# The pace of a frequency transform between the steps of a gated layer: a step clock that waits don't move, later ends for the first three transforms, and scatters of routing in threes

## The chip, the cores and the metric

One core of a Trainium2 chip runs the whole program in one launch. The metric is the device time of an execution in microseconds (us). The core has five engines that run side by side, each through its own list of instructions in order: TensorE (PE, matrix products), VectorE (DVE), ScalarE (ACT), GpSimd (POOL) and SyncE (SP, which here only issues DMAs). They wait for each other by semaphores. An instruction that waits holds everything behind it in its engine's list.

## The reference

The input x has 8 batches of 3072 tokens with 256 channels. Three stages follow each other:

```
X = rfft(x, axis=1)                       # along the tokens
Yr = Xr @ w_r - Xi @ w_i + b_r            # Yi the same with w_i, w_r, b_i
Y  = sign(Y) * max(|Y| - 0.01, 0)         # real and imaginary part by themselves
y  = irfft(Y)
z  = (sigmoid(y @ w_gate) * (y @ w_val)) @ w_out          # 256 -> 1536 -> 256
out = z; for tokens with z @ w_skip > 0:                  # routed to the best of 8 experts
    out += p_best * (relu(z @ w1[e]) @ w2[e])             # 256 -> 1024 -> 256
```

All matrix products are made of float16 high and low halves, three products for one.

## The kernel before

**Stages.** The program first sets up weights and makes the transform of batch 0 (the first 197 us). Then comes the main loop: 768 units, each one twelfth of the gated layer for one chunk of 384 tokens (8 batches x 8 chunks x 12). A unit is 12 matmuls for gate and value (L986, tile pg), the product of the two on DVE (h, then its low half hh), and 9 matmuls into the output (L1028, tile pz). After the loop come the experts' blocks (`Blocks`, tiles ph and py), 512 tokens or fewer at a time.

**What runs beside the units.** `moe_gen` yields once a unit. Between units, `build` gives turns to five other generators, its tasks:
- "attn": the transforms of batches 1 to 7 (`attn_gen`). Each has a stage of columns (x is scaled and split into xh, multiplied by c, stored through ah to asc) and one of 13 frequency groups (loaded as al; `freq` makes x, `mix` or `mix_pair` multiplies by wri and wse and shrinks, giving yn and by DMA yh, `inv` makes zh, stored to zsc).
- "y": `y_gen` finishes the inverse transform for one chunk, from zsc through zt, and leaves yT, which the gated layer's units of that chunk read.
- "route": `route` picks the experts of a batch's tokens and scatters an entry for each (the tile rent) into the list lst, 24 scatters a batch, by an indirect DMA that POOL issues (L1127). For the last batch it runs chunk by chunk, 3 scatters each; then come `full_table` and `rest_tables`, which say what the blocks work on.
- "prep": the experts' weights are scaled and split into float16 halves (pw, phl), 171 steps in all, the fill of the list lst among them.
- "start": the first blocks' loads, after the rest.

**What sets the order.** It is worked out while the program is built. Each task has a clock, counted in units. A step of a task may run when its clock is not past the unit; the one furthest behind goes first; and each unit has a budget of 2.0 us of estimated DVE and POOL or ACT work (BUDGET). After a step of "attn" its clock moves on by the step's estimated work times `span`, so that a transform should end 45 units (AHEAD) before its batch's own units begin. The other tasks move by a fixed number of units or by their work. A step may also set `k.due`, a unit before which its task isn't to go on: `settle` does (a maximum over all partitions is made by a matmul that rides with the next unit), and then the clock is raised to it, for "attn" as for the others.

When a task finds that what it needs isn't there, it names the other task, and `go` runs a step of that one at once, whatever budget or clock say. So y, when batch b isn't transformed (`while b not in k.made: yield "attn"`), and so `front` of the blocks, for a table.

The 8 chunks of y of a batch have due times too: LEAD and two chunks ahead of their use.

Of the kernel before, what the change touches and what calls it, by code (L numbers as in the profile page):

```python
# [16 lines left out]
NB, SEQ, D = 8, 3072, 256  # L17
# [6 lines left out]
NF = FF // 128  # L24
# [217 lines left out]
def task(gen):  # L242
    return [gen, []]


def step(k, r):

    k.V.sum = k.S.sum = k.T.sum = k.G.sum = 0.0
    todo, k.late = r[1], []
    for f in todo:  # L250
        f()
    got = next(r[0], -1)
    r[1] = k.late
    if got == -1 or isinstance(got, str):
        for f in r[1] if got == -1 else ():
            f()
        return got
    return max(k.V.sum + k.G.sum, k.S.sum)
# [647 lines left out]
def zt_load(k, b, c, boot=False):  # L906
    pool = k.sp0 if boot else k.yp
    zt = k.zt[b, c] = pool.tile([4 * NK, NJ, 2, D], F16, tag="zt", name=f"zt_{b}_{c}", bufs=1 if boot else 2)
    k.nc.sync.dma_start(zt, k.zsc[b][:, c * NJ:(c + 1) * NJ])
# [156 lines left out]
def route(k, b, t0, T):  # L1066

    nc, V, rp = k.nc, k.V, k.rp
    R = k.R[b][:, t0:t0 + T]
    L, S = R[:, :, 1:], R[:, :, 0]  # L1070
    tile_ = lambda tag, dt=F32, shape=None: rp.tile(shape or [128, T * NE], dt, tag=tag, name=f"{tag}_{b}_{t0}", bufs=1)
    tt = tile_("rt", shape=[128, 4, T])
    mx, sm, ac, gt = (tt[:, i] for i in range(4))
    et = lambda v: v.rearrange("p (e t) -> p e t", e=NE)
    te = lambda v: v.rearrange("p (e t) -> p t e", e=NE)
    bc = lambda v: v.unsqueeze(1).broadcast_to([128, NE, T])
    be = lambda v: v.unsqueeze(2).broadcast_to([128, NE, T])
    Le = L.rearrange("p t e -> p e t")
    dl, oh, w1, w2 = tile_("rdl"), tile_("roh"), tile_("rw1"), tile_("rw2")
    V.tensor_reduce(mx, L, axis=AX.X, op=ALU.max)  # L1080
    V.tensor_tensor(et(dl), Le, bc(mx), op=ALU.subtract)
    V.tensor_scalar(w1, dl, 0.0, None, op0=ALU.is_ge)
    k.S.activation(w2, dl, AF.Sigmoid)
    k.S.activation(dl, dl, AF.Sigmoid, scale=-1.0)
    yield
    V.reciprocal(dl, dl)
    V.tensor_tensor(dl, w2, dl, op=ALU.mult)
    V.tensor_tensor(et(w1), et(w1), be(k.rc[:, 0:NE]), op=ALU.mult)
    V.tensor_reduce(mx, te(w1), axis=AX.X, op=ALU.max)
    V.tensor_tensor(et(oh), et(w1), bc(mx), op=ALU.is_equal)  # L1090
    V.tensor_reduce(sm, te(dl), axis=AX.X, op=ALU.add)
    V.tensor_scalar(sm, sm, 1e-9, None, op0=ALU.add)
    V.reciprocal(gt, sm)
    V.tensor_scalar(ac, S, 0.0, None, op0=ALU.is_gt)
    oa = tile_("roa", F16)
    V.tensor_tensor(et(oa), et(oh), bc(ac), op=ALU.mult)
    yield
    ps = k.pa.tile([128, 512], F32, tag="pa", name="ps")
    W = T * NE
    nc.tensor.matmul(ps[:, :W], k.m16[:, 0], oa, start=True, stop=True)  # L1100
    nc.tensor.matmul(ps[:, W:2 * W], k.m16[:, 1], oa, start=True, stop=True)
    tot = tile_("rtot")
    V.tensor_copy(tot, ps[:, W:2 * W])
    V.tensor_tensor(w1, ps[:, :W], tot, op=ALU.subtract)
    yield
    V.memset(w2, 1.0)
    V.memset(et(w2)[:, :, 0:1], 0.0)
    V.tensor_tensor(et(tot)[:, :, 0], et(tot)[:, :, 0], k.base, op=ALU.add)
    inc = tile_("rdl")
    V.tensor_tensor_scan(inc, w2, tot, 0.0, op0=ALU.mult, op1=ALU.add)  # L1110
    V.tensor_copy(k.base, et(inc)[:, :, T - 1])
    yield
    V.tensor_tensor(w1, w1, inc, op=ALU.add)
    V.tensor_tensor(et(w1), et(w1), be(k.rc[:, NE:2 * NE]), op=ALU.add)
    V.tensor_tensor(w1, w1, oa, op=ALU.mult)
    V.tensor_reduce(sm, te(w1), axis=AX.X, op=ALU.add)
    yield
    V.tensor_scalar(ac, ac, -BIG, BIG, op0=ALU.mult, op1=ALU.add)
    idx = rp.tile([128, T], I32, tag="ridx", name="ridx", bufs=2)
    V.tensor_tensor(idx, sm, ac, op=ALU.add)  # L1120
    ent = rp.tile([128, T, 4], F32, tag="rent", name="rent", bufs=2)
    V.memset(ent[:, :, 3:4], 0.0)
    V.tensor_copy(ent[:, :, 0], gt)
    V.tensor_scalar(ent[:, :, 1:3], k.ids[:, t0:t0 + T, :], float(b * SEQ), None, op0=ALU.add)
    yield
    for t in range(T):
        nc.gpsimd.indirect_dma_start(  # L1127
            out=k.lst, out_offset=bass.IndirectOffsetOnAxis(ap=idx[:, t:t + 1], axis=0),
            in_=ent[:, t, :], in_offset=None, bounds_check=LROWS * BT - 1, oob_is_err=False,
        )  # L1130
        yield


def prep_gen(k):
# [247 lines left out]


def build(tc, d, nb=NB, nstat=NSTAT, dbg=None):
    PSTEP = 3.4 * nb / NB
    BUDGET = 2.0
    CARRY = 0.3
    LEAD = 9
# [2 lines left out]
    MIXAT = 9, 12, 13, 14, 15  # L1391
    SLACK = 1
    AHEAD = 44
    RATE = 0.9
    LAST = 36
    nc = tc.nc
    k = K()
# [5 lines left out]
    with ExitStack() as top, tc.manual_schedule():  # L1403
# [26 lines left out]
        total = step(k, ra)  # L1430
# [4 lines left out]
        while True:  # L1435
            w = step(k, ra)
# [28 lines left out]
        NU = NF * NC  # L1465
        END = nb * NU

        def ys():
            for b in range(nb):
                for c in range(1 if b == 0 else 0, NC):  # L1470
                    k.due = b * NU + (c - 2) * NF - LEAD
                    if c == 0:
                        k.due -= 6
                        yield
                        while b not in k.made:
                            yield "attn"
                        zt_load(k, b, 0)
                        k.due = b * NU - 2 * NF - LEAD
                    yield
                    yield from y_gen(k, b, c)  # L1480

        def attns():
            for b in range(1, nb):
                nonlocal span, spent, total
                k.due = k.due_ = max((b - 1) * NU - AHEAD, 0)
                yield
                span = (b * NU - AHEAD - 1 - k.due_) / total
                spent = 0.0
                if b == 1:
                    yield from mix_sums(k)  # L1490
                yield from attn_gen(k, b)
                total = spent
                k.made.add(b)
# [42 lines left out]
        tasks = {"y": ys, "attn": attns, "route": routes, "prep": lambda: prep_gen(k), "start": starts}  # L1536
        every = {"y": YSTEP, "attn": 0.0, "route": 3.2, "prep": PSTEP, "start": 1.0}
        run = k.run = {n: [task(g()), 0.0] for n, g in tasks.items()}
        k.made, room, u = {0}, 0.0, 0
        span = spent = 0.0  # L1540

        def go(n):
            nonlocal spent
            r = run[n]
            k.due = None
            w = step(k, r[0])
            if isinstance(w, str):
                go(w)
                return 0.0
            if w == -1:  # L1550
                del run[n]
                return 0.0
            if n == "attn":
                r[1] += w * span
                spent += w
            else:
                r[1] += max(every[n] if n != "route" or u < END - NU else 1.0, w * RATE)
            if k.due is not None:
                r[1] = max(r[1], float(k.due))
            return w  # L1560
# [29 lines left out]
        def front(j):  # L1590
            t, i = todo[j]
            while t not in k.tab:
                go("route")
            S[j] = bl.front(k.tab[t], i)
# [3 lines left out]
        def scale(j, steps):  # L1598
            if j not in scales:
                scales[j] = bl.scale(S[j])  # L1600
            for _ in range(steps):
                next(scales[j], None)

        for i in range(n):

            def during_first(f):
                if "route" in run and i == 0 and f in (0, 3):
                    go("route")
                if f == 1 and i + 2 < n:
                    front(i + 2)  # L1610
                if f == 6 and i + 2 < n:
                    bl.gather(S[i + 2], k.zs if todo[i + 2][0] else zs1)
                if f >= 2 and i + 1 < n:
                    scale(i + 1, 1)

            def during_second(q):
                if "route" in run:
                    go("route")
                if q == S[i].QT // 2 and i + 1 < n:
                    bl.transp(S[i + 1])  # L1620
                if q >= 2 and i + 2 < n and S[i + 1].QT < BT // 128:
                    scale(i + 2, PRE)

            bl.first(S[i], hp, during_first)
            bl.second(S[i], hp, during_second)
            del S[i]
# [37 lines left out]
```

## Time and profile before

| | us |
|---|---|
| median of 3 runs | 3648.33 (3648.04 to 3648.46) |
| the profiled execution | 3660.49 |
| its span, first to last instruction | 3658.7 |
| TensorE busy | 3398.8 (93%) |
| VectorE busy | 2349.7 (64%) |
| ScalarE busy | 1669.3 (46%) |
| GpSimd busy | 699.5 (19%) |
| mean granted clock of TensorE | 0.976 of full speed |

The profile is of one execution, 12 us above the median. TensorE's work is the same in every order of the steps; what is left of the span is its idle time, and time in which its clock is granted at half speed, which the profile shows behind idle time. A wait of another engine costs only if it reaches TensorE.

### The profile page before, as it was taken

The numbers are of one execution on the slowest core, as the hardware profiler recorded it, in microseconds if no ns is written. First come the engines' busy times: TensorE is split into PE (matmuls) and PEld (weight loads), VectorE is DVE, ScalarE is ACT, GpSimd is POOL, SyncE is SP. The second block draws the span as 40 slices with busy tenths as digits, with TensorE's granted clock in tenths as the row PEclk, the third lists the DMA queues.
The fourth block names the chain that finished last, engine by engine and source line by source line (L and its number), as shares of the span: only waits on it lengthen the run. The fifth ranks groups of instructions, "written<-read, shape, count | busy, mean of one in ns | idle before, by whom it ended". The sixth has DMA issues, their size and how long they took to land. (4 is left out here: it accounts for less than half of the span.)

```text
span 3658.7 us, 69199 instructions
## 1 busy us (share of the span) xinstructions
PE 3398.8 (93%) x26957; PEld 2384.6 (65%) x26958; DVE 2349.7 (64%) x5505; ACT 1669.3 (46%) x3276; POOL 699.5 (19%) x677
## 2 busy tenths in 40 slices
PE   4589979999999999999999999899999999899998
PEld 3456756676667666766776667667766666567675
DVE  7866656766776677667766766676645455565543
ACT  4544535454545454545554545454533443233332
POOL 3500100111111111211121102111210212333332
PEclk9889989999999999999999999999999999999999
DMA  6333223233323232323223322322211022344442
GB/s 166 114 103 106 80 86 101 72 91 90 89 77 90 77 99 82 88 74 99 83 79 87 97 87 69 90 76 69 65 46 36 27 85 70 121 148 142 160 151 102
DMA packets 230331, 336.07 MB, mean 92 GB/s; under 512 B 40705, under 2 KB 184835, under 8 KB 222736
## 3 DMA queue, kind: packets, MB, share of 16 engines
q1 hardware_dynamic: 213824, 305.31, 27.6%
q0 software_dynamic: 15744, 25.99, 2.3%
q8 instruction: 212, 3.47, 0.4%
q14 instruction: 119, 0.97, 0.1%
q10 hardware_dynamic: 432, 0.33, 0.0%
HBM read 177.86 MB, written 134.09 MB: 85 GB/s over the span
## 5 line engine op out<-in xcount | busy, mean ns | idle before, releaser
L986 PE MATMUL pg<-yT,wgv 128*128 128x384 f16 x9216 | 1657.6, 329 | 17.6 <-ACT sg L152 10.0
L986 PEld LDWEIGHTS <-wgv 128*128 128x128 f16 x9216 | 888.6, 99 | 565.4 <-issue 57.3
L1028 PE MATMUL pz<-wo,hh 128*128 128x265 f16 x6912 | 920.9, 278 | 14.9 <-DVE hh L152 11.5
L152 DVE TENSOR_TENSOR hh<-h,hh 128x384 f16<-128x384 f32 x768 | 447.0, 582 | 627.5 <-ACT hh L152 615.0
L1028 PEld LDWEIGHTS <-hh 128*128 128x128 f16 x6912 | 676.3, 98 | 209.8 <-DVE hh L152 17.0
L152 ACT ACTIVATE sg<-pg,ys 128x384 f32<-128x384 f32 x768 | 442.6, 576 | 558.2 <-PE pg L986 545.6
L152 DVE SCALAR_TENSOR_TENSOR h<-pg,sg 128x384 f32<-128x384 f32 x768 | 422.3, 550 | 4.5 <-PE pg L986 4.3
L152 ACT CAST hh<-h 128x384 f16<-128x384 f32 x768 | 386.6, 503 | 46.4 <-DVE h L152 45.8
L1127 POOL DMA_INDIRECT lst<-rent,ridx x192 | 200.9, 1046 | 447.0 <-DVE rent L152 233.8
L1352 PE MATMUL ph<-zT,we 128*128 128x512 f16 (+3 forms) x1344 | 273.5, 361 | 11.8 <-DVE h L152 11.0
L1372 PE MATMUL py<-we,h 128*128 128x256 f16 x2400 | 273.3, 273 | 4.7 <-issue 3.3
L1372 PEld LDWEIGHTS <-h 128*128 128x128 f16 x2400 | 233.1, 98 | 39.0 <-issue 6.6
L152 POOL TENSOR_TENSOR x<-sm,x 128x256 f16<-128x256 f32 x77 | 54.7, 710 | 1051.0 <-ACT x L152 844.1
L152 POOL TENSOR_TENSOR ah<-tmp,ah 128x512 f16<-128x512 f32 x64 | 73.9, 1154 | 866.0 <-ACT ah L152 649.4
L1352 PEld LDWEIGHTS <-we 128*128 128x128 f16 x1344 | 129.1, 99 | 146.4 <-issue 25.1
L152 PEld LDWEIGHTS <-x 128*128 128x128 f16 x1842 | 182.0, 100 | 41.8 <-issue 8.4
L152 ACT ACTIVATE h<-ph 128x512 f16<-128x512 f32 (+3 forms) x224 | 122.0, 547 | 172.2 <-PE ph L1352 165.1
L152 DVE SCALAR_TENSOR_TENSOR h<-ph,h 128x512 f16<-128x512 f32 (+3 forms) x224 | 140.6, 631 | 56.0 <-ACT h L152 54.1
L152 PE MATMUL ps<-yh,f 128*128 128x512 f16 (+1 forms) x312 | 87.2, 392 | 73.7 <-DMA yh<-yn 46.3
L152 DVE SCALAR_TENSOR_TENSOR og<-py,gr,zg 128x256 f32<-128x256 f32 x100 | 48.2, 483 | 162.3 <-PE py L1372 92.3
L1378 POOL DMA_INDIRECT out_dram<-og,ix x100 | 99.4, 994 | 240.9 <-DVE gr L152 65.8
L152 PE MATMUL ps<-wri,x 128*128 128x256 f16 x918 | 122.1, 279 | 9.5 <-DVE zh L152 3.8
(236 smaller groups left out, 3406.5 us busy)
## 6 DMA issues: line engine op xcount, KB each, us to landing
we<-w SPq DMA_DIRECT2D x56, 1024.0 KB
x<-in_x_dram SPq DMA_DIRECT2D x128, 192.0 KB
asc<-ah SPq DMA_DIRECT2D x256, 96.0 KB
al<-asc SPq DMA_DIRECT2D x192, 128.0 KB
zsc<-zh SPq DMA_DIRECT2D x192, 128.0 KB
zt<-zsc SPq DMA_DIRECT2D x64, 384.0 KB
zs<-zo SPq DMA_DIRECT2D x64, 384.0 KB
yh<-yn SPq DMA_DIRECT2D x308, 64.0 KB
```

The costliest lines, as they stand in the source:

```text
L152: return f(*a, **kw)
L986: nc.tensor.matmul(ps[:, :CT], k.wgv[:, t, g, a, f * 128:(f + 1) * 128], yT[:, t, w, :], start=n == 0, stop=n == 5)
L1028: nc.tensor.matmul(zs[(b, c)][t][:, :ZW], hh[:, a, t * 128:(t + 1) * 128], k.wo[:, f, w, :], start=f == 0 and i == 0, stop=f == NF - 1 and ...
L1127: nc.gpsimd.indirect_dma_start(out=k.lst, out_offset=bass.IndirectOffsetOnAxis(ap=idx[:, t:t + 1], axis=0), in_=ent[:, t, :], in_offset=No ...
L1352: k.nc.tensor.matmul(ps, st.w[0][:, a, t * FE + f * 128:t * FE + (f + 1) * 128], st.zT[:, t, w, :], start=m == 0, stop=m == 5,)
L1372: k.nc.tensor.matmul(ps[:, :D], st.h[f][:, a, q * 128:(q + 1) * 128], st.w[1][:, w, f * D:(f + 1) * D], start=n == 0, stop=n == 23,)
L1378: k.nc.gpsimd.indirect_dma_start(out=k.d.out, out_offset=bass.IndirectOffsetOnAxis(ap=st.ix[:, 0, q:q + 1], axis=0), in_=o[:, q], in_offse ...
```

## The change

Three things change; no instruction is added or dropped.

1. The clock of "attn" is a variable of its own, `plan`. It moves on by the work of each step. A wait raises the task's clock for the next step alone; the step after that is due by the plan again.
2. The ends that the plan aims at are a list: 21 units later than before for batch 1, 14 for batch 2, 7 for batch 3, and as before for the others. The start of a transform is the end of the one before. The chunks of y are due at the later of the old time and 8 + 10c units behind the end of their transform, for chunk c. PSTEP, the pace of "prep", goes from 3.4 to 3.9 units.
3. "route" issues three scatters in a step where it issued one, and the first block gives it four turns in its first half, not two.

```
-    PSTEP = 3.4 * nb / NB
+    PSTEP = 3.9 * nb / NB
+    RAMP = 21
+    GAP = 8
+    YGAP = 10
...
     for t in range(T):
+        if t % 3 == 0 and t:
+            yield
         nc.gpsimd.indirect_dma_start(
...
-        yield
+    yield
...
+        ends = [-GAP - YGAP] + [b * NU - AHEAD + max(RAMP - (b - 1) * RAMP // 3, 0) for b in range(1, nb)]
...
         def ys():
-                    k.due = b * NU + (c - 2) * NF - LEAD
+                    due = max(b * NU + (c - 2) * NF - LEAD, ends[b] + GAP + YGAP * c)
                     if c == 0:
-                        k.due -= 6
+                        k.due = due - 6
                         yield
                         while b not in k.made:
                             yield "attn"
                         zt_load(k, b, 0)
-                        k.due = b * NU - 2 * NF - LEAD
+                    k.due = due
...
         def attns():
-                k.due = k.due_ = max((b - 1) * NU - AHEAD, 0)
+                k.due = plan = float(max(ends[b - 1], 0))
                 yield
-                span = (b * NU - AHEAD - 1 - k.due_) / total
+                span = (ends[b] - 1 - plan) / total
...
             if n == "attn":
-                r[1] += w * span
+                plan += w * span
+                r[1] = plan
                 spent += w
...
-                if "route" in run and i == 0 and f in (0, 3):
+                if "route" in run and i == 0 and f % 2 == 0:
                     go("route")
```

**Where instructions move: the end of a transform, on DVE.** These rows are DVE's list at the end of the transform of batch 3, before. hh and h belong to the units; zh, yn, yf, yc and yh are the transform's last groups.

```order
L152 TENSOR_TENSOR hh<-h_14958,hh 128x384
L152 SCALAR_TENSOR_TENSOR h_14990<-pg,sg 128x384
L152 SCALAR_TENSOR_TENSOR zh<-ps,zh 128x2x256
L152 TENSOR_TENSOR yn<-yf,yn 128x2x256
L152 SCALAR_TENSOR_TENSOR yf<-ps,bs_10304,bb_12279 128x256
L152 TENSOR_SCALAR yc<-yf,bs_10304 128x256
L152 TENSOR_TENSOR yf<-yf,yc 128x256
L152 TENSOR_TENSOR yh<-yf,yh 128x256
L152 SCALAR_TENSOR_TENSOR zh<-ps,zh 128x2x256
L152 SCALAR_TENSOR_TENSOR zh<-ps,zh 128x256
L152 TENSOR_TENSOR hh<-h_14990,hh 128x384
```

The same place now:

```order
L152 TENSOR_TENSOR yn<-yf,yn 128x2x256
L152 SCALAR_TENSOR_TENSOR yf<-ps,bs_10444,bb_12319 128x256
L152 TENSOR_SCALAR yc<-yf,bs_10444 128x256
L152 TENSOR_TENSOR yf<-yf,yc 128x256
L152 TENSOR_TENSOR hh<-h_14912,hh 128x384
L152 SCALAR_TENSOR_TENSOR h_14974<-pg,sg 128x384
L152 SCALAR_TENSOR_TENSOR yT_7_14932<-y_14714,ys_7_14849,yT_7_14932 128x2x384
L152 TENSOR_TENSOR yh<-yf,yh 128x256
L152 TENSOR_TENSOR hh<-h_14974,hh 128x384
L152 SCALAR_TENSOR_TENSOR h_15007<-pg,sg 128x384
L152 SCALAR_TENSOR_TENSOR zh<-ps,zh 128x2x256
```

Between yn, whose DMA makes yh, and the zh of the inverse that reads that yh, no unit stood before; now two pairs of hh and h do. At the ends of batches 1 and 2 it is one pair.

**The scatters, on POOL.** POOL's list while batch 1 is routed and batch 3 is in its frequency groups (x is the low half of a group's spectrum, yf its bias sum), before:

```order
L1127 DMA lst<-rent,ridx 197120x4
L152 TENSOR_TENSOR x<-sm,x 128x2x128
L152 TENSOR_TENSOR yf<-bg_10309,com 128x512
L1127 DMA lst<-rent,ridx 197120x4 x2
L152 TENSOR_TENSOR x<-sm,x 128x2x128
```

and now:

```order
L1129 DMA lst<-rent,ridx 197120x4 x3
L152 TENSOR_TENSOR x<-sm,x 128x2x128
L152 TENSOR_TENSOR yf<-bg_10449,com 128x512
L1129 DMA lst<-rent,ridx 197120x4 x6
L152 TENSOR_TENSOR x<-sm,x 128x2x128
```

Where one or two scatters stood between a yf and the next x, three stand, and at six places in the program six.

**The first blocks, on DVE.** Before, in block 4, with h the experts' hidden layer, og a block's output and the others rows of routing the last chunk:

```order
L152 SCALAR_TENSOR_TENSOR og<-py,gr,zg 128x256 x2
L152 SCALAR_TENSOR_TENSOR h_40818<-ph,h_40818 128x512
L152 TENSOR_REDUCE rt_21_40821<-R_36315 128x3
L152 TENSOR_TENSOR rdl_21_40822<-R_36315,rt_21_40821 128x24
L152 TENSOR_SCALAR rw_7_21_40824<-rdl_21_40822 128x24
L152 RECIPROCAL rdl_21_40822<-rdl_21_40822 128x24
L152 TENSOR_TENSOR rdl_21_40822<-rw_7_21_40825,rdl_21_40822 128x24
L152 TENSOR_TENSOR rw_7_21_40824<-rw_7_21_40824,rc 128x24
```

Now, in block 0, the end of the same chunk's routing:

```order
L152 SCALAR_TENSOR_TENSOR og<-py,gr,zg 128x256
L152 TENSOR_SCALAR rt_21_39715<-rt_21_39715 128x3
L152 TENSOR_TENSOR ridx<-rt_21_39715 128x3
L152 MEMSET rent 128x3
L152 COPY rent<-rt_21_39715 128x3
L152 TENSOR_SCALAR rent<-ids 128x3x2
L152 SCALAR_TENSOR_TENSOR og<-py,gr,zg 128x256
```

Before, 60 rows of routing and tables stand between one h and the next there; now a step of routing stands between two og, some blocks ahead of the one that asks for the table.

## Rows read from the trace of the kernel before

**Rows 1.** The page: busy us, share and instructions of PE and PEld.

```profile
PE 3398.8 (93%) x26957; PEld 2384.6 (65%) x26958; DVE 2349.7 (64%) x5505; ACT 1669.3 (46%) x3276; POOL 699.5 (19%) x677
```

**Rows 2.** Windows: from:to, length, busy us (count) per engine, PEclk, DMA share, GB/s.

```profile
200.00:700.00 500.00, 450.34 (x3663) 311.69 (x3662) 335.03 (x763) 238.78 (x461) 42.68 (x42) 0.94 0.31 89
700.00:2800.00 2100.00, 2029.94 (x16405) 1431.48 (x16404) 1401.36 (x3128) 1037.41 (x2058) 327.10 (x313) 0.99 0.28 81
```

**Rows 3.** PE's waits, 197 to 3650 us: total us, times, longest us.

```profile
PE ps L152 <- DMA yh<-yn: 46.3, 12, 7.8
PE ps L152 <- DVE xh L152: 18.3, 12, 3.4
PE pz L1028 <- DVE hh L152: 11.5, 12, 4.2
...
PE ps L152 <- DMA zt<-zsc: 4.5, 1, 4.5
```

**Rows 4.** Windows around the ends of the seven transforms, and their sum.

```profile
472.00:508.00 36.00, 19.50 (x116) 11.87 (x114) 18.03 (x31) 10.89 (x22) 3.38 (x4) 0.81 0.24 66
846.00:860.00 14.00, 8.95 (x57) 5.73 (x56) 7.92 (x18) 3.81 (x9) 0.96 (x1) 0.88 0.22 62
1209.00:1225.00 16.00, 10.44 (x57) 6.13 (x55) 6.55 (x13) 3.38 (x8) 1.00 (x1) 0.79 0.24 65
1564.00:1583.00 19.00, 11.16 (x66) 6.83 (x65) 8.01 (x15) 3.95 (x8) 5.16 (x5) 0.82 0.24 64
1928.00:1945.00 17.00, 9.77 (x49) 5.54 (x50) 7.18 (x14) 3.48 (x7) 3.99 (x5) 0.80 0.22 58
2288.00:2307.00 19.00, 10.03 (x67) 6.59 (x66) 8.55 (x16) 4.98 (x10) 5.18 (x5) 0.82 0.24 64
2653.00:2665.00 12.00, 8.54 (x53) 5.51 (x51) 5.52 (x11) 2.66 (x6) 4.85 (x5) 0.86 0.28 78
sum 133.00, PE 78.40 PEld 48.20 DVE 61.77 ACT 33.14 POOL 24.52; mean PE 11.20 PEld 6.89 DVE 8.82 ACT 4.73 POOL 3.50
```

**Rows 5.** Timeline at batch 3's end: start us, busy us, instruction, [idle before <-releaser].

```profile
1203.59 2.11 PE L986 MATMUL pg<-yT,wgv 128*128 128x384 f16 x12
...
1205.54 1.19 PE L1028 MATMUL pz<-wo,hh 128*128 128x265 f16 x9
...
1211.63 0.68 DVE L152 TENSOR_TENSOR yn<-yf,yn 128x512 f16<-128x512 f32 x1
...
1217.22 2.08 PE L152 MATMUL ps<-yh,f 128*128 128x512 f16 x6 [5.56 <-DMA yh<-yn]
```

**Rows 6.** Windows around other waits: yT, xh (two), sg, hh (two), route.

```profile
284.00:296.00 12.00, 8.24 (x58) 4.67 (x54) 6.43 (x11) 4.26 (x10) 1.15 (x1) 0.72 0.13 36
...
522.00:534.00 12.00, 7.58 (x58) 4.59 (x56) 6.07 (x16) 5.80 (x11) 1.15 (x1) 0.72 0.38 103
608.00:634.00 26.00, 19.84 (x157) 12.37 (x156) 13.85 (x26) 12.70 (x23) 2.31 (x2) 0.87 0.40 119
652.00:660.00 8.00, 5.50 (x27) 3.27 (x27) 6.14 (x29) 3.38 (x6) 0.00 (x0) 0.79 0.00 0
1374.00:1380.00 6.00, 3.92 (x28) 2.51 (x27) 4.27 (x13) 1.82 (x4) 0.00 (x0) 1.00 0.00 0
2143.00:2155.00 12.00, 7.82 (x39) 4.70 (x38) 8.75 (x18) 1.31 (x3) 0.10 (x1) 0.72 0.10 33
3162.00:3183.00 21.00, 12.76 (x42) 4.67 (x40) 16.24 (x75) 5.21 (x11) 7.27 (x8) 0.76 0.32 106
```

**Rows 7.** Timeline of POOL while scatters go out, columns as in rows 5.

```profile
1129.83 1.03 POOL L1127 DMA_INDIRECT lst<-rent,ridx  x1 [2.99 <-DMA lst<-rent,ridx]
...
1142.95 1.29 POOL L1127 DMA_INDIRECT lst<-rent,ridx  x1 [0.16 <-issue]
1153.82 0.66 POOL L152 TENSOR_TENSOR x<-sm,x 128x256 f16<-128x256 f32 x1 [9.58 <-ACT x L152]
...
1204.52 0.99 POOL L1127 DMA_INDIRECT lst<-rent,ridx  x1 [0.16 <-issue]
1206.89 0.97 POOL L1127 DMA_INDIRECT lst<-rent,ridx  x1 [1.38 <-DMA lst<-rent,ridx]
...
1209.26 1.00 POOL L1127 DMA_INDIRECT lst<-rent,ridx  x1 [1.40 <-DMA lst<-rent,ridx]
```

More of the change, by code (lines that the diff above doesn't have):

```diff
@@ L1483, in attns @@
             for b in range(1, nb):
-                nonlocal span, spent, total
-                k.due = k.due_ = max((b - 1) * NU - AHEAD, 0)
+                nonlocal span, spent, total, plan
+                k.due = plan = float(max(ends[b - 1], 0))
                 yield
-                span = (b * NU - AHEAD - 1 - k.due_) / total
+                span = (ends[b] - 1 - plan) / total
                 spent = 0.0
@@ L1539, in build @@
         k.made, room, u = {0}, 0.0, 0
-        span = spent = 0.0
+        span = spent = plan = 0.0
         def go(n):
-            nonlocal spent
+            nonlocal spent, plan
             r = run[n]
```

## Prediction

> **What bounds the kernel now.** I read the page first: TensorE (PE) is busy 93% of a span of 3658.7 us [rows 1]. Nothing else is near that, so a change that moves work without adding any can only save what PE loses: idle time, and the time at half clock that follows it. The stages are next [rows 2]. From 200 to 700 us PE is idle for 49.7 us and its mean granted clock is 0.94; from 700 to 2800 us it is idle 70.1 us of 2100. Third, the waits of PE over the main loop and the blocks [rows 3]: the largest, 46.3 us in 12 waits, is the inverse transform waiting for the DMA that brings yh. The gaps in order of time show where these are: not spread, but one cluster at the end of each transform, seven in all. I put a window around each [rows 4]: 133 us, PE busy 78.4, idle 54.6.
>
> The order says why. At these places seven to seventeen steps of the transform stand one behind the other with no hh and h of the gated stage between them (front part, first pair of order rows). This is the forced path: y asks for batch b before the transform has made it, and go runs "attn" until it is made. The timeline of one end shows it [rows 5]: yn is ready at 1212.31 (1211.63 + 0.68), and the matmul that reads yh starts at 1217.22, after 5.56 us of idle. So yn to usable yh is 4.9 us, and nothing lies on PE to cover it.
>
> **The change part by part.** No instruction is added or removed: only their order, and so what covers what. Durations are those of the profiled execution (3660.5 us, 12.2 above the median of 3648.3); the saving is taken from that and subtracted from the median, since a 0.3% rescaling of 55 us is nothing.
>
> *1. The clock of the transform is not pushed back.* Before, each settle sets due to the next unit and the clock keeps that; after, plan goes on as if it hadn't waited, so the steps behind it follow sooner. With the later ends of the first three and y's due times behind these, no transform is forced any more; the order has hh and h between the last steps at all seven ends. What goes: idle 54.6 us, and clock. In each window the loss by the clock is at most its length by one minus its granted clock: 6.8 + 1.7 + 3.4 + 3.4 + 3.4 + 3.4 + 1.7 = 23.8 us. Part of the half clock falls on idle PE; PE is busy 59% of these windows, so I take 14. Together 68.6 us [rows 4].
>
> What is late next: the same yh. From the fourth transform's end (batch 3) on, two units stand between yn and its inverse. A unit is 12 gate and value matmuls (2.11 us) and 9 of the output (1.19): 3.3 us [rows 5]. Two are 6.6, above the 4.9 needed: hidden. At the first two ends (batches 1 and 2) it is one unit, so 1.6 us remain, with as much again by the clock: 2 x 3 = 6 us. Then y's first zt load of batch 1: it stands as close to its matmul as before, and cost 4.5 us there [rows 3], of which the wait for the stores of zh goes because those are now some units old. It lies in the first window; I leave 3 us of it. So part 1 gives 68.6 - 6 - 3 = 59.6, with 68.6 and 34 (half of each end left) as ends.
>
> *2. y's chunks of batch 0 spread, at a lower rate of asking.* The third yT was made too late: around 287 us PE is idle 3.8 us, at 0.72 clock, 12 x 0.28 x 0.69 = 2.3 us [rows 6]. In the new order some 16 us of PE work stand between yT and its first use, where 3 stood. Saved: 6.1; ends 0 and 6.1.
>
> *3. Routing in fewer steps.* In the last batch three scatters go out in one step, so each chunk needs 7 steps and not 9, and block 0 takes four and not two of them. Before, at block 4 the table of the rest was not made and 17 steps were forced there: one run of routing rows on VectorE (DVE) between two h of a block (third pair of order rows). Window 3162 to 3183: PE idle 8.2, clock 0.76, 21 x 0.24 x 0.61 = 3.1 us: 11.3 us [rows 6]. After, no step is forced there. I take 9, since the same DVE rows now stand inside other blocks; ends 0 and 11.3.
>
> *4. What gets worse: steps closer together.* Steps that catch up after a wait come two or three to a unit. Two costs are seen before. First, columns whose matmul stands directly behind the split of xh: five such places before, six after. The window of one: idle 4.4, clock 12 x 0.28 x 0.63 = 2.1; of two: idle 6.2, clock 26 x 0.13 x 0.76 = 2.6; 5.1 us each [rows 6]. So minus 5; ends 0 and minus 15, if two more of the short distances stop being covered. Second, DVE bursts. Adding up DVE's durations for each unit of the order and comparing with PE's, DVE falls over 3 us behind at three places before (652, 1377 and 2148 us in the trace) and at seven after, four of them where the bias rows bb of a transform come in the same unit as the lo half of a yT. The three cost 2.5 + 1.2, 2.1, and 4.2 + 2.2 us: 12.2, or 4 each [rows 6]. Four more: minus 16; I take 12, ends 0 and 24.
>
> *5. Scatters in threes on GpSimd (POOL).* Each is 0.99 us of POOL and waits for the landing of the one before, 1.38 us [rows 7]. Threes take 0.16 + 2.97 + 2.76 = 5.9 us. Behind them on POOL stand the lo half of x and then the bias sum yf, for which DVE waits at the head of its queue, with hh behind it. The cover: between two yf POOL is free from 1142.79 to 1153.82, 11.0 us. A three fits. At six places, one a batch, the order has two threes together: 13.0 us, 2 over. So 0 to 6 x 2 = 12; x has three units to spare before its matmul, so I take 2.
> The Trainium skill speaks against this part (DMA: Bandwidth & Descriptors, Anatomy of one DMA — SWDGE (gpsimd) path): a DMA issued from GpSimd has a fixed cost of about 2.0 us, most of it the receipt of the write. The waits of 1.38 us are shorter and one of 2.99 us longer. By that page's figure six scatters would take about 16 us, 5 over at six places, and the sum would be about 28 us smaller at worst; no run here shows a six.
>
> PSTEP 3.9 makes prep end near unit 663, not 578, before its users at 700 and later, beside a PE that is 97% busy in that part of the loop [rows 2]: nothing.
>
> Sum: 59.6 + 6.1 + 9 - 5 - 12 - 2 = 55.7 us. 3648.3 - 55.7 = 3592.6: 3593 us, 1.5% faster.
>
> **Rivals.**
> *The ends stay half open.* The yh DMAs are four issues on SP's queue, behind weight stores, loads of x and the zt that y now spreads over the same time. If that queue makes 4.9 us into 8, two units no longer cover it, and 34 us of part 1 are left: 3648 - 30 = 3618. For it: 5.56 us is not the longest such wait, 7.8 is [rows 3]. Against: at distances of three units the trace shows no wait.
> *DVE becomes the bound in bursts.* All of part 4 at its upper ends, 15 + 24, and nothing from part 3: 59.6 + 6.1 - 39 - 2 = 25 us, 3623. For it: the first two transforms now run with hardly a unit under the budget. Against: DVE is busy only 67% from 200 to 2800 us [rows 2], so a burst is worked off within a unit or two.
> *No change.* Both at once leave about nothing: 3645.
> *Slower: the scatters hold POOL.* If every scatter waited 2.99 us, as one did [rows 7], a six would take 0.16 + 5.94 + 14.95 = 21.0 us, 10 over the free 11. Six of these are 60 us, handed by POOL to DVE through yf and by DVE to PE through hh, with 2 us of half clock each (14 over seven ends): 72 us. Against the gain without part 5, 57.7, that is 14 us slower: 3662. It decides from a wait of about 2.5 us (30 scatters' waits, less 29.4 us of cover, and 12 us of clock reach 57.7). Against it: a three still fits, and the back to back waits in the trace are 1.38 and 1.40.
>
> **How the numbers follow.** Forecast 0.68; ends half open 0.10, bursts 0.11, no change 0.05, slower 0.06. Under 0.2% (7 us) a measurement of this kernel can't be told from no change. Faster: 0.68 + 0.10 + 0.11 = 0.89; same 0.05; slower 0.06. The low end of the range takes all of part 1 to 3 and half of part 4 and 5's costs: 68.6 + 6.1 + 11.3 - 8 = 78, taken as 80: 3568. Above, it takes in both faster rivals: 3630. Outside are 0.11 above and some 0.08 below.
>
> **What would show it.** In the new profile: the PE wait for yh from 46 us to under 10, and none over 4 us; no window at a transform's end with a clock under 0.9; no wait for yT near 290 us; PE's share from 200 to 700 us above 94%. No idle of 4 us on PE in the first blocks. If part 4 is larger, PE's waits for hh and xh rise above the 11.5 and 18.3 us of before [rows 3]. If the scatters hold POOL, DVE shows waits for yf of over 4 us. The prediction is wrong if PE's idle moves from yh to hh or xh in the same amount, or if the waits at the ends stay.

## The result, and the profile after

3598.3 us (3595.8 to 3600.8, 4 runs) against 3648.4 before: a ratio of 0.9863, 95% interval 0.9846 to 0.9880, 50 us faster. The forecast was 3593. The profiled execution took 3600.8 us, 59.7 less than that of before; the latter lay 12 us above its median and this one 2.5, so some 10 of the 59.7 us are not the change's.

PE is busy about as long, in a shorter span (page; then windows as in [rows 2]):

```profile
PE 3384.8 (94%) x26957; PEld 2379.7 (66%) x26958; DVE 2352.7 (65%) x5505; ACT 1664.2 (46%) x3276; POOL 698.3 (19%) x677
```

```profile
200.00:700.00 500.00, 478.86 (x4002) 335.61 (x4001) 356.28 (x805) 254.91 (x499) 56.20 (x54) 0.99 0.32 93
700.00:2800.00 2100.00, 2032.60 (x16367) 1429.87 (x16365) 1408.96 (x3165) 1032.55 (x2054) 325.87 (x313) 0.99 0.28 81
```

From 200 to 700 us the idle time falls from 49.7 to 21.1 us and the clock rises from 0.94 to 0.99. From 700 to 2800 us PE is idle 67.4 us, hardly less than 70.1: there other idle time has taken the place of what went. PE's waits show part of it (total, times, longest, as [rows 3]):

```profile
PE pz L1028 <- DVE hh L152: 22.7, 18, 2.2
PE ps L152 <- DVE xh L152: 20.7, 17, 3.1
PE pg L986 <- ACT sg L152: 12.9, 11, 3.7
...
PE ps L152 <- DMA yh<-yn: 3.9, 3, 2.8
```

The waits for yh are down from 46.3 to 3.9 us, that for zt is gone, and those for hh have doubled from 11.5. Windows around the seven ends, the first three and the sum, against [rows 4]:

```profile
470.00:506.00 36.00, 35.30 (x259) 24.71 (x258) 24.91 (x50) 18.13 (x38) 3.73 (x3) 1.00 0.34 100
812.00:830.00 18.00, 15.18 (x111) 10.48 (x109) 10.35 (x25) 6.67 (x14) 0.00 (x0) 1.00 0.51 157
1148.00:1164.00 16.00, 16.00 (x118) 11.29 (x117) 11.24 (x27) 6.77 (x14) 0.00 (x0) 1.00 0.20 58
...
sum 134.00, PE 129.93 PEld 91.50 DVE 85.84 ACT 61.78 POOL 8.14; mean PE 18.56 PEld 13.07 DVE 12.26 ACT 8.83 POOL 1.16
```

PE is idle for 4.1 us where it was for 54.6, and the granted clock is 1.00 in all seven windows. The end of batch 3, as [rows 5]:

```profile
1150.39 0.68 DVE L152 TENSOR_TENSOR yn<-yf,yn 128x512 f16<-128x512 f32 x1
1150.75 2.11 PE L986 MATMUL pg<-yT,wgv 128*128 128x384 f16 x12
...
1152.70 1.19 PE L1028 MATMUL pz<-wo,hh 128*128 128x265 f16 x9
...
1153.73 2.11 PE L986 MATMUL pg<-yT,wgv 128*128 128x384 f16 x12
...
1155.68 1.19 PE L1028 MATMUL pz<-wo,hh 128*128 128x265 f16 x9
1156.71 0.81 PE L152 MATMUL ps<-yh,f 128*128 128x512 f16 x3
```

The matmul that reads yh comes 5.6 us after yn, without a wait: two units lie between. They take less than the 6.6 us of the prediction, which added 2.11 and 1.19 us although the two groups of matmuls overlap: here one unit begins 2.98 us after the other.

The blocks, from the last unit to PE's end, before (first row) and after (second):

```profile
3060.00:3646.00 586.00, 563.24 (x4194) 390.31 (x4191) 324.78 (x884) 186.68 (x361) 203.21 (x203) 0.99 0.39 138
```

```profile
3024.00:3586.00 562.00, 553.29 (x4180) 388.15 (x4178) 319.36 (x826) 185.32 (x356) 197.17 (x198) 1.00 0.41 144
```

Some 22 us are saved here (the first window begins 1.6 us further ahead of the last unit): idle falls from 22.8 to 8.7 us, and most of the rest is PE's busy time, at a clock of 1.00 for 0.99.

### The profile page after: what moved, and what is told of

It is laid out like the page before. It is cut to its first block, busy times and chain, and to the rows that moved or that the text cites. A ratio compares the mean times of both kernels' runs of the same rounds, so it can differ in the third digit from the quotient of the medians.

```text
span 3598.9 us, 69199 instructions
## 1 busy us (share of the span) xinstructions
PE 3384.8 (94%) x26957; PEld 2379.7 (66%) x26958; DVE 2352.7 (65%) x5505; ACT 1664.2 (46%) x3276; POOL 698.3 (19%) x677
## 5 line engine op out<-in xcount | busy, mean ns | idle before, releaser
L986 PE MATMUL pg<-yT,wgv 128*128 128x384 f16 x9216 | 1654.7, 328 | 16.6 <-ACT sg L152 12.9
L1028 PE MATMUL pz<-wo,hh 128*128 128x265 f16 x6912 | 922.6, 278 | 26.8 <-DVE hh L152 22.7
L1310 POOL DMA_INDIRECT zg<-zs,ix x100 | 102.3, 1023 | 131.3 <-DVE zh L152 38.4
```

Source lines behind the costliest of these rows:

```text
L986: nc.tensor.matmul(ps[:, :CT], k.wgv[:, t, g, a, f * 128:(f + 1) * 128], yT[:, t, w, :], start=n == 0, stop=n == 5)
L1028: nc.tensor.matmul(zs[(b, c)][t][:, :ZW], hh[:, a, t * 128:(t + 1) * 128], k.wo[:, f, w, :], start=f == 0 and i == 0, stop=f == NF - 1 and ...
L1310: nc.gpsimd.indirect_dma_start(out=st.z[:, q, :], out_offset=None, in_=zs, in_offset=bass.IndirectOffsetOnAxis(ap=st.ix[:, 1, q:q + 1], ax ...
```

## The experiments

Every kernel was timed in three rounds beside the kernel before on its chip; the ratios are to that, and the medians of before differ by 0.3% from chip to chip, so only ratios are compared. Times in us are ratios times 3648.4.

| run | step clock | ends, y's due times | scatters | ratio (95%) |
|---|---|---|---|---|
| after | new | new | threes | 0.9863 (0.9846 to 0.9880) |
| clock_alone | new | old | singles | 1.0113 (1.0097 to 1.0130) |
| ends_alone | old | new | singles | 0.9818 (0.9801 to 0.9834) |
| no_clock | old | new | threes | 0.9804 (0.9788 to 0.9821) |
| old_y | new | ends new, y old | threes | 0.9982 (0.9973 to 0.9992) |
| oc_noramp | old | ends old, y new | threes | 1.0079 (1.0063 to 1.0096) |
| route_alone | old | old | threes | 1.0053 (1.0036 to 1.0070) |
| route_com | old | old | threes, com apart | 0.9973 (0.9964 to 0.9983) |
| singles | new | new | singles, but last batch | 0.9803 (0.9787 to 0.9820) |
| old_clock_singles | old | new | singles, but last batch | 0.9782 (0.9766 to 0.9799) |
| after_com | new | new | threes, com apart | 0.9795 (0.9779 to 0.9812) |
| oc_com | old | new | threes, com apart | 0.9757 (0.9741 to 0.9773) |
| after_com_gap_bb | new, two more dues | new | threes, com apart | 0.9702 (0.9686 to 0.9719) |

clock_alone and ends_alone have two turns of routing in block 0, all others below four; PSTEP is 3.4 in clock_alone, ends_alone, route_alone and route_com, and 3.9 elsewhere. Neither was changed by itself.

### Which part opens the ends

**clock_alone**, against before (cut; the lines that give `plan` and `span` their values are left out):

```
-                r[1] += w * span
+                plan += w * span
+                r[1] = plan
```

> The kernel before with the step clock alone: plan is not pushed back by waits; ends, due times of y, PSTEP and routing as before. Theory A (the clock opens the seven ends, the rest is secondary): the PE wait for yh falls from 46 us to under 10, and the time to about 3595 to 3605 us. Theory B (the order shows no forced transform, but y forced 11 times between units 49 and 170, because the transforms of batches 1 and 2, which no wait holds up now, take the budget first): about 60 us saved at the ends, 11 forced chunks of y at 6 us (what the late yT near 287 us cost) to 10 us each lost, so 3648 - 60 + 66 to 110 = 3654 to 3698 us, and PE waits for yT of 30 us or more.

1.0113: slower, inside theory B's range. The ends are open: no wait for yh is left among PE's. But y comes too late (PE's waits):

```profile
PE ps L152 <- DVE xh L152: 34.0, 13, 3.6
PE pg L986 <- ACT yT L152: 29.1, 12, 5.0
...
PE pm L188 <- DVE pp L152: 16.3, 7, 4.4
PE pg L986 <- DVE yT L152: 11.2, 13, 3.8
PE ps L152 <- DMA zt<-zsc: 8.8, 1, 8.8
```

yT, pp and zt are all steps of y, made at the unit that needs them: 65 us, more than the waits for yh had been (46.3). The part that the change is named for costs 41 us by itself.

**no_clock**, against after:

```
-                plan += w * span
-                r[1] = plan
+                r[1] += w * span
```

> The kernel after with the old clock: each wait pushes the clock of the transform back again; later ends, due times of y, PSTEP and routing as after. Theory A (the clock is what opens the ends): the forced ends come back, 3630 to 3648 us. Theory C (the lateness was handed on from one transform to the next, and the later first three ends with y's due times behind them break that chain; the order forces one end alone, batch 1's, 8 steps, and has 3 columns directly behind their split, not 6): the six other ends stay open, so 8 to 10 us are lost at the end of batch 1 and up to 15 us won at the columns: 3585 to 3608 us, PE wait for yh under 12 us.

0.9804, clearly below after, and some 8 us below theory C's range.

```profile
PE ps L152 <- DMA yh<-yn: 9.2, 5, 3.6
```

So the ends are open without the new clock too, as theory C has it: the clock opens them by itself (clock_alone), but it isn't needed, and it costs 0.6% here.

**ends_alone**: no_clock with PSTEP 3.4, single scatters and f in (0, 3).

> The later ends and y's due times alone: clock pushed back by waits, PSTEP, single scatters and two turns in block 0 as before. The order forces batch 1's end (8 steps) and, in the blocks, 17 steps of routing. Theory C (these two do the work): six of seven ends open, some 50 us saved of 3648, nothing saved in the blocks: 3590 to 3605 us. Theory D (and threes cost some 30 us in the loop, as the run with the routing alone suggests, against 10 to 18 won in the blocks): 3570 to 3595 us, PE waits for hh and sg below those of the kernel after.

0.9818, 3582 of 3648: these two edits alone give more than the whole change. That is in D's range and below C's, and PE waits less for hh (22.7 us in after) and for sg (12.9):

```profile
PE pg L986 <- ACT sg L152: 11.4, 18, 1.8
PE pz L1028 <- DVE hh L152: 11.1, 11, 2.7
```

From no_clock it differs by the routing and PSTEP, and the two times can't be told apart: the blocks, between the first and the last matmul of ph, take 575.5 us here and 551.5 there, so most of what the routing wins in them goes in the loop.

**old_y**, against after:

```
-                    due = max(b * NU + (c - 2) * NF - LEAD, ends[b] + GAP + YGAP * c)
+                    due = b * NU + (c - 2) * NF - LEAD
```

> The kernel after with y's old due times: clock, later ends, PSTEP and routing as after. The order forces the ends of batches 1 (27 steps), 2 (9) and 3 (4) and no other. Theory A and C both: three forced ends at 17 + 6 us for the first and 6 to 7 for each of the others come back, 25 to 35 us: 3623 to 3633 us. If y's due times were only of use for the late yT of batch 0 (6 us): 3600 to 3606 us.

0.9982, 3642 of 3648: 44 us worse than after, more than the 25 to 35 expected. y asks for batch 1 too early and 27 steps are forced at once; of the waits for yh, 10.5 us lie between 300 and 500 us.

```profile
PE ps L152 <- DMA yh<-yn: 16.5, 8, 5.4
```

With the new clock, later ends without later asking leave almost nothing of the gain; with the old clock that was not run.

**oc_noramp**, against no_clock:

```
-    RAMP = 21
+    RAMP = 0
```

> Old clock, y's new due times, routing of after, and the ends of the first three transforms where they were before. The order forces the ends of batches 2 to 7 (14 to 18 steps each). Theory C as a chain (a transform that is finished by force leaves its clock behind, and the next starts late; only room at the first ones breaks it): 6 ends at 7 to 9 us, and the late yT: 0.980 x 3648 + 48 to 60 = 3625 to 3637, ratio 0.993 to 0.998. If the due times of y alone were enough: 0.980 to 0.984.

1.0079: the mechanism as expected, its price far too low. Six ends are forced again, and they cost 100 us against no_clock where 48 to 60 were expected: beside yh, PE now waits for zh. No such wait stands from 300 to 700 us, where batch 1's end lies.

```profile
PE ps L152 <- DMA yh<-yn: 43.5, 16, 5.8
PE ps L152 <- DVE zh L152: 21.9, 10, 2.7
```

Together: the later first ends with y's due times behind them are enough for the gain in the loop (ends_alone). It goes without the later ends on the old clock (oc_noramp) and without y's due times on the new one (old_y); the other two pairings were not run. That lateness goes on from one transform to the next is inferred from the order on the old clock: with the later ends it forces batch 1's end alone, without them those of batches 2 to 7. In old_y, on the new clock, it forces the first three and no later one, as if nothing were handed on there.

### What the scatters in threes do

**route_alone**: before with the two edits of the routing.

> The kernel before with the routing alone: scatters in threes, four turns in block 0. The forced ends stay. Theory of the prediction: 9 us saved in the first blocks (PE waits for roa and h there go), 0 to 12 lost to POOL, so 3637 to 3645 us. Rival (the scatters hold POOL): 3650 to 3710 us, with DVE waits for yf over 4 us.

1.0053, slower: the rival's side, at its low end. The blocks win as much as in after (551.5 us between the first and the last matmul of ph, 573.9 before), so the loop loses some 40 us. But DVE's waits for yf did not grow (44.4 us, 3.9 at most, before):

```profile
DVE yf L152 <- POOL yf L152: 32.2, 15, 3.1
```

POOL's timeline in this kernel, at two steps of scatters that stand together, and what follows on ScalarE and PE:

```profile
718.62 1.18 POOL L1129 DMA_INDIRECT lst<-rent,ridx  x1 [0.17 <-issue]
721.18 0.98 POOL L1129 DMA_INDIRECT lst<-rent,ridx  x1 [1.38 <-DMA lst<-rent,ridx]
...
728.53 0.97 POOL L1129 DMA_INDIRECT lst<-rent,ridx  x1 [1.62 <-DMA lst<-rent,ridx]
732.23 0.97 POOL L1129 DMA_INDIRECT lst<-rent,ridx  x1 [2.73 <-DMA lst<-rent,ridx]
733.21 0.69 POOL L152 TENSOR_TENSOR x<-sm,x 128x256 f16<-128x256 f32 x1
```

```profile
733.93 0.47 ACT L152 ACTIVATE com<-ps,bs 128x256 f32<-128x256 f32 x1 [3.78 <-POOL x L152]
734.46 2.20 PE L152 MATMUL ps<-wse,x 128*128 128x256 f16 x12 [3.11 <-ACT com L152]
```

Six scatters hold POOL for 14.6 us here; the six places in after take 14.2 to 16.3. Then comes x, and only when x has been read from sm can ScalarE write com, for com is allocated under sm's tag with one buffer (`tag="sm", name="com", bufs=1` in `mix_pair`). So ScalarE stands, with the sigmoid and the high half of hh behind com, and PE waits for its PSUM bank. ScalarE's wait, in the kernels before, route_alone, after and singles:

```profile
ACT com L152 <- POOL x L152: 53.0, 60, 1.4
```

```profile
ACT com L152 <- POOL x L152: 85.3, 63, 6.3
```

```profile
ACT com L152 <- POOL x L152: 80.6, 62, 7.3
```

```profile
ACT com L152 <- POOL x L152: 52.2, 58, 1.4
```

**singles**, against after, and **old_clock_singles**, the same against no_clock:

```
-        if t % 3 == 0 and t:
+        if t and (t % 3 == 0 or T > 3):
```

> The kernel after with single scatters for batches 0 to 6 and threes only where the last batch is routed chunk by chunk; four turns in block 0 kept. Theory D (threes hold POOL; x is late, and com on ScalarE, which shares the buffer of sm with it, then waits): 10 to 25 us faster than after, 3573 to 3590 us, and no PE wait for com over 1 us. Rival E (the loss with the routing alone came of the forced ends and of chance bunching of steps): within 5 us of after, 3593 to 3603 us.

> Old clock, later ends, y's new due times, threes only for the last batch, four turns in block 0. The best of the parts if D holds: the run without the new clock (3580 us) less 10 to 25, so 3555 to 3570 us; the order has 2 columns directly behind their split and one forced end (8 steps). If E holds: 3575 to 3583 us.

0.9803, 22 us faster than after, though the blocks lose some of what they had won: 566.9 us between the first and the last matmul of ph, for 551.6 in after. The last scatter goes out 56 us after the blocks begin, not 32. So in the loop the threes cost some 35 us, by these two numbers. With the old clock 0.9782 against 0.9804, 8 us and less than D expected; the intervals overlap.

**route_com**, against route_alone, **after_com** against after, **oc_com** against no_clock:

```
-        com = k.gp.tile([128, D], F32, tag="sm", name="com", bufs=1)
+        com = k.gp.tile([128, D], F32, tag="com", name="com", bufs=1)
```

> The kernel before with the routing of after (3671 us by itself), and com in a buffer of its own instead of sm's only one, so that ScalarE's com no longer waits for POOL's x. Theory D by way of com: PE's waits for com (10.3 us in 5) go, those for hh and sg fall from 37 to about 25 us, and 15 to 25 us come back: 3646 to 3656 us. If POOL is held but reaches PE by yf and DVE: com's waits go, DVE's waits for yf rise, and the time stays within 6 us of 3671. Rival E: nothing changes, waits for com included in other names.

> The kernel after with com in a buffer of its own, threes kept. After stands at 0.986 of before; with single scatters in the loop it was 0.980. If the threes cost by way of com alone: 0.978 to 0.982 of before (22 us of 3648 come back), as with singles. If there is another way (yf and DVE): 0.984 to 0.986. PE's waits for com (2.2 us) are small in after, so the gain would have to show in waits for hh and sg (41 us in after), by ScalarE no longer held.

> Old clock, later ends, y's new due times, threes, and com in its own buffer. Without that buffer 0.980. If threes cost by com there too: 0.974 to 0.978. If the old clock's order has hardly any place where a three meets com: 0.979 to 0.982.

0.9973 from 1.0053, 0.9795 from 0.9863, 0.9757 from 0.9804: 29, 25 and 17 us for a buffer, with the scatters as they are. So the wait for com's buffer is the main way of the loss: in after 25 us of some 35. The buffer was not run with single scatters, where com waited for x too (53.0 us before, 1.4 at most), so how much of the 25 us belongs to the threes is not shown. In after_com ScalarE's wait for POOL's x is no longer among its largest, and PE's for sg falls from 12.9 to 4.9 us; that for hh stays:

```profile
PE pz L1028 <- DVE hh L152: 23.1, 19, 2.2
PE ps L152 <- DVE xh L152: 20.6, 17, 3.1
...
PE pg L986 <- ACT sg L152: 4.9, 7, 1.6
```

In singles it is 20.0, so the threes are not the cause of most of it.

### What bunched steps cost

**after_com_gap_bb**, against after_com (cut):

```
             load(c + 3)
+            at = k.unit
             yield
+            if c in (0, NC - 2, NC - 1) and at == k.unit:
+                k.due = k.unit + 1
+                yield
             cols(c, ((k.pa, "pa"),) * 2)
...
     V.tensor_scalar(col(10), col(7), -LAM, None, op0=ALU.mult)
+    if b:
+        k.due = k.unit + 1
+        yield
     bb = ...
```

and the same three lines once more behind bb.

> The kernel after with com in its own buffer, a unit between the low half of xh and its columns (the first and the last two of a transform) and the bias rows bb in three steps a unit apart. The clock that is not pushed back takes these dues without falling behind: the order forces nothing and has no column directly behind its split (after has 6). Prediction part 4 (each such column 5 us, bursts 4 us each): 25 to 30 us for xh, 8 to 16 for bb below after_com: 0.968 to 0.974 of before; PE waits for xh from 20 us to under 10. Rival (the waits move to the next step): within 5 us of after_com.

0.9702, 34 us below after_com and the fastest of all, 109 us below before. The waits, to hold against the 23.1 and 20.6 us of after_com:

```profile
PE pz L1037 <- DVE hh L152: 14.7, 15, 3.1
PE ps L152 <- DVE xh L152: 7.9, 15, 1.3
```

and PE in the long stretch, in after_com (first row) and here (second), idle for 59.4 and 41.5 us:

```profile
700.00:2800.00 2100.00, 2040.60 (x16453) 1437.55 (x16451) 1424.29 (x3193) 1039.53 (x2067) 329.40 (x319) 0.99 0.28 81
700.00:2800.00 2100.00, 2058.53 (x16713) 1453.75 (x16711) 1441.79 (x3271) 1049.90 (x2094) 333.62 (x323) 1.00 0.28 82
```

xh's share and that of bb were not run apart. The new clock may pay here, since the added dues don't push it back; the same edits on the old clock were not run, so that isn't shown.

## Why the prediction was right

The time came out 5 us from the forecast, in part by luck: two sizes were off in opposite directions, and the part named first is not what gained the time.

- *Bound.* Right: the seven clusters of rows 4 were the largest removable loss. They went, with the clock's dips in them.
- *Part 1, the ends.* 59.6 us expected; idle time at the ends fell by 50.5 us, and with the 14 that the prediction estimated for the clock, now 1.00, that is 64.5. Two units did cover the 4.9 us from yn to yh at batch 3, with 5.6 us and not 6.6. One unit was too short at batch 2 (2.8 us); at batch 1 no wait remained, and zt's, of which I had left 3 us, was gone. What failed is the share of the clock: the prediction put the clock that isn't pushed back first, with the later ends and y's due times beside it. The clock alone opens the ends but makes the kernel 1.1% slower, as y then comes late, and without it the change is 0.6% better. The later ends and y's due times win the time.
- *Part 2.* Right: the wait for yT near 287 us is gone (PE is idle for 0.03 us from 280 to 300).
- *Part 3, the blocks.* 9 us expected, some 22 measured. The one window that I took is gone whole, and with it smaller waits of the other blocks that had routing rows in them.
- *Part 4, bunched steps.* 17 us expected. Waits for xh stayed (18.3 to 20.7), those for hh rose by 11, in more and smaller gaps than the 4 us each I took: 18, none over 2.2. The columns behind their split and the bursts at bb were the right places: spacing both won 34 us.
- *Part 5, the scatters.* 2 us expected, 25 measured by the buffer and some 35 by single scatters. The sixes of after took 14.2 to 16.3 us, 13.0 by the sum's rows. By my estimate from the fixed cost that the Trainium skill gives (DMA: Bandwidth & Descriptors, Anatomy of one DMA — SWDGE (gpsimd) path) a six was about 16 us; the trace reaches that in two of the six. The failed step is "x has three units to spare": its own matmul has, but com waits for x too, for a buffer, and I followed only yf. That the sixes overrun the free 11 us was right, the way to PE was not, nor the sign "DVE shows waits for yf of over 4 us" (3.6 at most in after).
- *The sum.* From the execution profiled, parts 1 to 3 gave 64.5 + 6.1 + 22 = 93 us, where 75 were expected, and 93 - 60 = 33 were lost again, where 19 were expected. How the 33 divide between parts 4 and 5 isn't shown. PSTEP, put at nothing, was not run by itself.

The rival "the scatters hold POOL" was no rival but a part of the result: true, at a third to a half of its 72 us. "Bursts" likewise: waits for hh rose, but the time stayed 25 us below its 3623.

## What to carry to other kernels

A pacing change can be checked before it runs: list for each DMA or split how much of the bound engine's work stands between producer and consumer in the new order, and compare with the latency in the trace. Work grouped into one step on an idle engine isn't free: follow every reader of what stands behind it, and every tile that shares a buffer with what it reads. When a bundle helps, time its parts; here two of three, run by themselves, made the kernel slower.

## What the runs showed that was not expected

Scatters that wait for each other hold POOL far longer than the 0.97 us of one suggests: in the row of six shown above, 6.0 us of busy time took 14.6. The wait for the landing of the one before isn't steady. This is one of the sixes of after, 16.2 us in all:

```profile
1800.26 0.99 POOL L1129 DMA_INDIRECT lst<-rent,ridx  x1 [0.15 <-issue]
1802.67 0.97 POOL L1129 DMA_INDIRECT lst<-rent,ridx  x1 [1.41 <-DMA lst<-rent,ridx]
1806.43 0.97 POOL L1129 DMA_INDIRECT lst<-rent,ridx  x1 [2.79 <-DMA lst<-rent,ridx]
1809.07 0.97 POOL L1129 DMA_INDIRECT lst<-rent,ridx  x1 [1.66 <-DMA lst<-rent,ridx]
1813.18 0.97 POOL L1129 DMA_INDIRECT lst<-rent,ridx  x1 [3.14 <-DMA lst<-rent,ridx]
1815.52 0.97 POOL L1129 DMA_INDIRECT lst<-rent,ridx  x1 [1.37 <-DMA lst<-rent,ridx]
```

It doesn't take a long row for that. In the kernel before, the second of two scatters waited as long:

```profile
1724.57 0.97 POOL L1127 DMA_INDIRECT lst<-rent,ridx  x1 [3.63 <-DMA lst<-rent,ridx]
```

The sum took 1.38 us, near the shortest of these waits, for all of them.
